# Transposing u in 32x32 blocks on VectorE and through memory instead of on TensorE, in the last layer of a retention and feed-forward kernel

## The chip, the cores and the metric

One core of a Trainium2 chip. The core has a matrix engine (TensorE; in the profile PE, and PEld for its weight loads), VectorE (DVE), ScalarE (ACT), GpSimd (POOL) and SyncE (SP, which only issues DMAs), an on-chip memory of 128 partitions (SBUF), accumulation banks that TensorE writes (PSUM), and 16 DMA engines that move data between SBUF and DRAM (HBM). The metric is the time of one execution on the device in microseconds, the median of several runs.

## The reference

Three layers follow each other. Retention over 4 batches of 8 heads gives 3072 tokens of 512 values; a first feed-forward layer follows, and then the layer that this change touches:

```python
def _moe2_ref(x, w_in, w_out, g_ln) -> np.ndarray:   # x 3072 x 512, w_in 512 x 1024, w_out 1024 x 512
    h = x @ w_in
    h_max = np.max(h, axis=-1, keepdims=True)
    e = np.exp(h - h_max)
    sm = e / (np.sum(e, axis=-1, keepdims=True) + 1e-09)
    solu = h * sm
    mu = np.mean(solu, axis=-1, keepdims=True)
    var = np.mean((solu - mu) ** 2, axis=-1, keepdims=True)
    ln = (solu - mu) / np.sqrt(var + 1e-06) * g_ln
    return (ln @ w_out).astype(np.float32)
```

All data is float32. The kernel multiplies float32 operands as pairs of rounded halves: each operand is split into a high part and a rest, and three products (high by high, high by rest, rest by high) are summed.

## The kernel before

The kernel is written so that TensorE's order stands in the code; the order on the other engines is made by a scheduler when the program is built, and each engine then runs its list strictly in that order, waiting where an operand is not there. The DMAs that SyncE issues are such a list too, and so are those that ScalarE issues in between its computations.

The first two layers fill the time up to about 606 us. The last layer works on 24 tiles of 128 tokens (P = 128), in 12 pairs; pair j holds the tiles 2j and 2j + 1, called the even and the odd tile below. For each pair:

- h2, the product with w_in, is formed in seven partial products (a scheme that saves one of eight) of 6 matmuls each, 42 in all. `part` issues them; `keep2` and `add_half` bring the sums from PSUM into a tile `hn` of 128 x 1024 and find its maximum. The odd tile's `hn` is complete after P4, the even one's after P3, the last of the seven.
- `soft` makes u from it: the exponential on ACT (line 951), the product h·exp with its row sum on DVE (line 953), the mean subtracted from it on DVE (line 955), the sum of squares on ACT (line 957), and some one-column operations for the scale.
- `trans` turns u: 8 transposes of 128 x 128 on TensorE into PSUM (line 976, tiles `ptr`), a rounded copy `uh` on ACT (line 978), and the rest `ul` on DVE (line 979). After it the 1024 inner values lie on the partitions, in 8 blocks of 128.
- `outp` multiplies by w_out: 24 matmuls of 512 columns (line 990), the eviction with the scale on ACT (line 996) and the output's DMA, issued by ACT (line 998).

`load_y` fetches the layer's input `yl` from DRAM two or three pairs ahead (line 469, issued by SyncE); `sum_y` and `split_y` form the sums and the rounded parts of it on POOL and ACT (lines 476, 483 to 486 and 499).

The pair 0 is computed inside the last steps of the layer before. Then a loop over j from 1 to 12 puts TensorE's work in this order: P1 and P2 of pair j, the transposes of the odd tile of pair j - 1, P6 and P5, the transposes of its even tile, P7, the first half of the odd tile's output, P4 and P3, the rest of that output, and the even tile's output. In j = 12 there is no pair left and only transposes and outputs remain.

Of the kernel before, what the change touches and what calls it, by code (L numbers as in the profile page):

```python
# [60 lines left out]
C_MASK = C_HALF + 1  # L61
C_IDENT = C_MASK + D
C_END = C_IDENT + P

# [6 lines left out]
def constants():  # L71
    gamma = 1.0 - 2.0 ** (-5.0 - np.arange(H, dtype=np.float64))
    i = np.arange(P, dtype=np.float64)
    out = np.zeros((P, C_END), np.float64)
    out[:, C_IDENT : C_IDENT + P] = np.eye(P)
    for c in range(NC):
        out[:, C_VS + c * H : C_VS + (c + 1) * H] = gamma[None, :] ** -(c * P + i[:, None] + 1)
    out[:, C_HALF] = -0.5
    out[:, C_MASK : C_MASK + D] = np.tile(i[:D, None] <= i[None, :D], (2, 1))

    tab = np.zeros((NC, P, NP * P), np.float64)
    of_q = tab.reshape(NC, 2, D, NP, P)
    for p in range(NP):
        for h in range(2):
            for c in range(NC):
                of_q[c, h, :, p, :] = gamma[2 * p + h] ** (c * P + i + 1) / np.sqrt(D)
    return out.astype(np.float32), tab.astype(np.float32)
# [3 lines left out]
def body(ctx: ExitStack, tc, z, w_in, w_out, w_in2, w_out2, g_ln, cst, tab, out):  # L91
# [19 lines left out]

    con = cpool.tile([P, C_IDENT], F32, name="con")
    gl = cpool.tile([P, NF2], F32, name="gl")
# [5 lines left out]
    gd = {s: yd.tile([P, NF1, SB], F32, name=f"gd{s}") for s in range(2, NSB)}  # L119
    y1d = [yd.tile([P, B, NK, P], F32, name=f"y1d{s}") for s in range(NSB)]  # L120


# [499 lines left out]
    load_tab(0)  # L622
    nc.scalar.dma_start(out=con, in_=cst[:, :C_IDENT])
    load_half(0, 1)
# [283 lines left out]
    w2p = ctx.enter_context(tc.tile_pool(name="w2p", bufs=7))  # L908
    bp = ctx.enter_context(tc.tile_pool(name="bp", bufs=1))
    sp = ctx.enter_context(tc.tile_pool(name="sp", bufs=3))  # L910
    ident = bp.tile([P, P], F32, name="ident")
    nc.sync.dma_start(out=ident, in_=cst[:, C_IDENT:])
    uc, ut, sc2, po_of = {}, {}, {}, {}

# [31 lines left out]
    def soft(i, h, last):  # L946
# [7 lines left out]
        nc.vector.tensor_scalar(us, us, -1.0 / FF2, None, ALU.mult)  # L954
        nc.vector.tensor_scalar(hn, ex, us, None, ALU.add)
        ssq = sp.tile([P, 1], F32, tag="ssq", name="ssq")
        nc.scalar.activation(ex, hn, AF.Square, accum_out=ssq)

# [7 lines left out]
        uc[i], sc2[i] = hn, sc  # L966

    def trans(i):
        u = uc.pop(i)
        uh = t4([P, NF2, P], F32R, "uh")  # L970
        ul = t4([P, NF2, P], F32R, "ul")
        for half in range(2):
            pt_ = ps_t.tile([P, 4, P], F32, tag="tr", name="ptr")
            for q in range(4):
                f = 4 * half + q
                nc.tensor.transpose(pt_[:, q, :], u[:, f * P : (f + 1) * P], ident)  # L976
            hs = slice(4 * half, 4 * half + 4)
            nc.scalar.copy(uh[:, hs, :], pt_)
            nc.vector.tensor_tensor(ul[:, hs, :], pt_, uh[:, hs, :].bitcast(F32), ALU.subtract)
        ut[i] = (uh, ul)  # L980

    def outp(i, fs):
        uh, ul = ut[i]
        if fs[0] == 0:
            po_of[i] = ps_o.tile([P, DM], F32, tag="o", name="po")
        po = po_of[i]
        for f in fs:
            bh, bl = dec2.w[f]
            for n, (a, b) in enumerate(((uh, bh), (uh, bl), (ul, bh))):
                nc.tensor.matmul(  # L990
                    po, a[:, f, :], b, start=f == 0 and n == 0, stop=f == NF2 - 1 and n == 2
                )
        if fs[-1] < NF2 - 1:
            return
        ob = t2([P, DM], F32, "ob")
# [45 lines left out]
    for n, (s, f) in enumerate(steps):  # L1041
# [19 lines left out]
        if s == NSB - 1:  # L1061
# [14 lines left out]
            if f == 12:  # L1076
                split_y(1)
            if f == 14:
                sum_y(2)
# [3 lines left out]

    ps_2 = ctx.enter_context(tc.tile_pool(name="ps_2", bufs=4, space=PSUM, reuse_waits="tile"))
    ps_t = ctx.enter_context(tc.tile_pool(name="ps_t", bufs=2, space=PSUM, reuse_waits="tile"))
    ps_o = ctx.enter_context(tc.tile_pool(name="ps_o", bufs=2, space=PSUM, reuse_waits="tile"))
    NJ = NTT // 2
    bank_of[:] = [(ps_2, "h2")]
    load_y(3)
    with tc.manual_schedule(engines={mybir.EngineType.PE}):  # L1090
        for j in range(1, NJ + 1):
            if j + 1 < NJ:
                split_y(j + 1)
            a, b = 2 * j - 1, 2 * j - 2
            pair = Pair(j) if j < NJ else None

            def parts2(*ms):
                for m in ms if pair else ():
                    pair.part(m)

            parts2(P1, P2)
            trans(a)
            parts2(P6, P5)
            trans(b)
            if j + 2 < NJ:
                sum_y(j + 2)
            if j + 3 < NJ:
                load_y(j + 3)
            parts2(P7)
            outp(a, range(4))  # L1110
            parts2(P4, P3)
            outp(a, range(4, NF2))
            outp(b, range(NF2))

# [54 lines left out]
```

## Time and profile before

| | us |
|---|---|
| median of 3 runs | 875.61 (874.99 to 877.58) |
| the profiled execution's own time | 874.27 |
| its span in the trace | 872.5 |
| TensorE busy in the span | 840.5 (96%) |
| VectorE, ScalarE, GpSimd busy | 540.0, 438.8, 303.6 |
| TensorE's granted clock, mean over the span | 0.993 of full speed |

The span runs from the first to the last instruction of the traced execution; the 1.8 us around it belong to the start and the end of the program. A matmul that is queued behind another overlaps it in the trace, so the mean duration of one is longer than the distance from one to the next; the distances are what counts for the time.

### The profile page before, as it was taken

Reading aid. Unit: us, or ns where it says so; the run is one execution under the profiler, and the core shown is the slowest. Engines: PE = TensorE matmul, PEld = TensorE weight load, DVE = VectorE, ACT = ScalarE, POOL = GpSimd, SP = SyncE. Lnnn points to the kernel's source line nnn. Section 1 sums busy time; section 2 is a strip of 40 time slices with the busy share of each in tenths; the row PEclk is TensorE's granted clock in tenths of the full one; section 3 lists DMA queues with packets and bytes.
Section 4 is the critical chain, followed back from the end, with each engine's and each line's share of the span. In section 5 each row is a group of like instructions: output and inputs, shape, how many; then the busy total and the mean of one; then the engine's idle time right before and its main releaser. Section 6 shows DMA issues by size and latency. Waiting matters only on the chain.

```text
span 872.5 us, 16642 instructions
## 1 busy us (share of the span) xinstructions
PE 840.5 (96%) x6488; PEld 693.8 (80%) x6488; DVE 540.0 (62%) x1023; ACT 438.8 (50%) x868; POOL 303.6 (35%) x304
## 2 busy tenths in 40 slices
PE   5799999999999899999999999999899999999997
PEld 5678888888877687887788888888788888888886
DVE  3788876999768766224465977555455545544441
ACT  4656643646545455445453445435555555555442
POOL 4521100271634257343300430235644444444200
PEclk9999999999999899999999999999999999999999
DMA  9668754335899528935676455522111111100001
GB/s 363 252 236 298 241 203 152 113 134 213 305 361 331 181 80 283 410 143 173 242 276 211 152 199 208 188 105 76 58 49 49 49 48 48 45 30 25 22 17 47
DMA packets 66462, 144.34 MB, mean 165 GB/s; under 512 B 6608, under 2 KB 19024, under 8 KB 66384
## 3 DMA queue, kind: packets, MB, share of 16 engines
q1 hardware_dynamic: 58032, 128.28, 41.7%
q10 hardware_dynamic: 8352, 15.00, 4.6%
q8 instruction: 51, 0.84, 0.4%
q14 instruction: 27, 0.22, 0.1%
HBM read 94.50 MB, written 48.76 MB: 164 GB/s over the span
## 4 chain that ended last, share of the span: by engine, by line
PE 82%; DMA 5%; DVE 4%; issue 3%; POOL 3%; ACT 2%; SPq 0%; ACTq 0%; POOLq 0%; DVEq 0%
PE py L378 28%; PE po L990 15%; PE ph L751 12%; PE ph L926 12%; PE ph L353 8%; PE ptr L976 2%; DMA z<-z 2%; PE out L229 2%; PE sc L229 2%; DMA raw<-w_in 1%; POOL hs L769 1%; DMA wcd<-wch 1%; DMA wf<-wod 1%; POOL yls L476 1%; DVE wf L145 1%
## 5 line engine op out<-in xcount | busy, mean ns | idle before, releaser
L378 PE MATMUL py<-gp,w 128*128 128x512 f32 x768 | 175.4, 389 | 0.0
L378 PEld LDWEIGHTS py<-gp,w 128*128 128x128 f32 x768 | 144.2, 188 | 29.9
L990 PE MATMUL po<-w,uh 128*128 128x512 f32 x384 | 118.6, 390 | 0.0
L769 POOL TENSOR_TENSOR hs<-hs,th 128x512 f32<-128x512 f32 x48 | 66.5, 1389 | 97.1 <-ACT th L767 86.9
L476 POOL TENSOR_TENSOR yla<-yl,yha 128x256 fp32r<-128x256 f32 x36 | 40.0, 1140 | 130.7 <-ACT yha L499 130.7
L990 PEld LDWEIGHTS po<-w,uh 128*128 128x128 f32 x384 | 72.1, 188 | 14.9
L353 PE MATMUL ph<-xh,w 128*128 128x512 f32 x256 | 82.2, 395 | 0.9 <-DVE w L155 0.9
L378 PE MATMUL py<-gh,w 128*128 128x512 f32 x256 | 79.3, 390 | 0.3 <-ACT gh L366 0.3
L990 PE MATMUL po<-w,ul 128*128 128x512 f32 x192 | 74.9, 390 | 0.0
L154 ACT CAST w<-wf 128x512 fp32r<-128x512 f32 x70 | 43.0, 619 | 58.4 <-DVE wf L145 47.7
L926 PE MATMUL ph<-w,yhs 128*128 128x512 f32 x192 | 61.3, 400 | 0.0
L767 ACT ACTIVATE th<-hs 128x512 f32<-128x512 f32 x48 | 30.3, 631 | 61.2 <-DVE hs L777 54.7
L162 DVE TENSOR_TENSOR gp<-g,gp 128x512 fp32r<-128x512 f32 x64 | 48.7, 772 | 19.6 <-ACT gp L161 19.4
L155 DVE TENSOR_TENSOR w<-wf,w 128x512 fp32r<-128x512 f32 x70 | 51.3, 738 | 15.1 <-ACT w L154 14.3
L751 PE MATMUL ph<-xh,wch 128*128 128x512 f32 x140 | 57.3, 409 | 1.6 <-DVE hs L777 1.6
L353 PEld LDWEIGHTS ph<-xh,w 128*128 128x128 f32 x256 | 48.0, 188 | 11.8 <-DVE w L155 1.3
L378 PEld LDWEIGHTS py<-gh,w 128*128 128x128 f32 x256 | 48.0, 188 | 10.6 <-ACT gh L366 0.7
L751 PE MATMUL ph<-xl,wch 128*128 128x512 f32 x140 | 55.4, 396 | 0.0
L751 PE MATMUL ph<-xh,wcl 128*128 128x512 f32 x140 | 55.2, 395 | 0.0
L777 DVE TENSOR_TENSOR hs<-ph,part 128x512 f32<-128x512 f32 x48 | 33.0, 687 | 35.3 <-PE ph L751 20.9
L951 ACT ACTIVATE ex<-hn,nm 128x1024 f32<-128x1024 f32 x24 | 27.7, 1153 | 53.2 <-DVE nm L941 52.4
L751 PE MATMUL ph<-xh,wc 128*128 128x512 f32 x168 | 53.2, 391 | 1.2 <-ACT part L761 0.6
(124 smaller groups left out, 1777.6 us busy)
## 6 DMA issues: line engine op xcount, KB each, us to landing
z<-z SPq DMA_DIRECT2D x48, 512.0 KB, 7.2
g<-gd SPq DMA_DIRECT2D x64, 256.0 KB, 5.4
raw<-w_in SPq DMA_DIRECT2D x24, 512.0 KB, 6.2
raw<-w_out SPq DMA_DIRECT2D x24, 512.0 KB, 4.5
gd<-hs SPq DMA_DIRECT2D x48, 256.0 KB, 3.8
y1d<-ysb SPq DMA_DIRECT2D x24, 256.0 KB, 3.5
wc<-wcd SPq DMA_DIRECT2D x12, 512.0 KB, 6.6
yl<-y1d SPq DMA_DIRECT2D x12, 512.0 KB, 4.0
```

The costliest lines, as they stand in the source:

```text
L154: pin(nc.scalar.copy(hi, wf), fixed)
L155: pin(eng.tensor_tensor(lo, wf, hi.bitcast(F32), ALU.subtract), fixed)
L162: eng.tensor_tensor(o, src, h.bitcast(F32), ALU.subtract)
L229: pin(nc.tensor.matmul(o, a, b, start=True, stop=True, skip_group_check=True), held[0])
L353: nc.tensor.matmul(ph, a[:, k, :], x, start=n == 0, stop=n == 3 * NK - 1), s < 2
L378: nc.tensor.matmul(py[e], a[:, cols], x, start=f == 0 and n == 0, stop=f == NF1 - 1 and n == 2)
L476: nc.gpsimd.tensor_tensor(out[:, at], a[:, at], b[:, at], op)
L751: nc.tensor.matmul(ph, a, x, start=first and n == 0, stop=n == 5, skip_group_check=True)
L769: eng.tensor_tensor(g, h, th, ALU.subtract)
L777: nc.vector.tensor_tensor(h, ph, part, ALU.add)
L926: nc.tensor.matmul(ph, x[:, r, :], w, start=first and n == 0, stop=n == 5, skip_group_check=True)
L990: nc.tensor.matmul(po, a[:, f, :], b, start=f == 0 and n == 0, stop=f == NF2 - 1 and n == 2)
```

## The change

TensorE's transposes go. In `soft` ACT now subtracts the mean (an Identity activation with the mean as its bias, in place of DVE's line 955), and the sum of squares is taken from the unshifted product with the same bias. DVE then transposes the tile within blocks of 32 x 32 (`nc.vector.transpose`, into the buffer `ex`), and SyncE stores it to a DRAM tensor `ud` (512 KB, 4 KB contiguous from each partition). A new step `turn` reads it back into `hn` with another order of rows: each destination partition gathers 32 runs of 32 values (128 bytes each), 4096 runs for a tile. `trans` then makes `uh` and `ul` from that in SBUF, with one copy on ACT and one subtraction on DVE of 128 x 1024 each. The rows of w_out and g_ln are reordered on the host to match, and the identity matrix goes.

The order on TensorE is new too: all 42 matmuls of pair j run together, and behind them the 48 output matmuls of pair j - 1. At the end the matmuls of pairs 10 and 11 follow each other, and then the outputs of the pairs 9, 10 and 11. The PSUM banks of the transposes go to h2 (6 instead of 4).

```diff
--- before.py
+++ after.py
...
@@ -118,6 +116,7 @@
     wcd = [[yd.tile([P, 4, 256], F32, name=f"wcd{j}_{i}") for i in range(4)] for j in range(NJ1)]
     gd = {s: yd.tile([P, NF1, SB], F32, name=f"gd{s}") for s in range(2, NSB)}
     y1d = [yd.tile([P, B, NK, P], F32, name=f"y1d{s}") for s in range(NSB)]
+    ud = [yd.tile([P, NF2 * P], F32, name=f"ud{i}") for i in range(NTT)]
 
 
     def raw_load(src):
...
@@ -952,9 +948,12 @@
         us = sp.tile([P, 1], F32, tag="us", name="us")
         nc.vector.scalar_tensor_tensor(ex, hn, 1.0, ex, ALU.mult, ALU.mult, accum_out=us)
         nc.vector.tensor_scalar(us, us, -1.0 / FF2, None, ALU.mult)
-        nc.vector.tensor_scalar(hn, ex, us, None, ALU.add)
+        nc.scalar.activation(hn, ex, AF.Identity, bias=us)
         ssq = sp.tile([P, 1], F32, tag="ssq", name="ssq")
-        nc.scalar.activation(ex, hn, AF.Square, accum_out=ssq)
+        nc.scalar.activation(ex, ex, AF.Square, bias=us, accum_out=ssq)
+
+        nc.vector.transpose(ex, hn)
+        nc.sync.dma_start(out=ud[i], in_=ex)
 
         nc.vector.tensor_scalar(ssum, ssum, 1e-9, -1.0, ALU.add, ALU.mult)
         nc.vector.reciprocal(ssum, ssum)
@@ -965,33 +964,28 @@
         nc.gpsimd.tensor_tensor(sc, sc, ssum, ALU.mult)
         uc[i], sc2[i] = hn, sc
 
+    def turn(j):
+        for i in (2 * j + 1, 2 * j):
+            nc.sync.dma_start(
+                out=uc[i].rearrange("p (c i b) -> p c i b", c=NF2, i=B),
+                in_=ud[i].rearrange("(i a) (g c b) -> (a g) c i b", i=B, g=4, c=NF2),
+            )
+
     def trans(i):
         u = uc.pop(i)
-        uh = t4([P, NF2, P], F32R, "uh")
-        ul = t4([P, NF2, P], F32R, "ul")
-        for half in range(2):
-            pt_ = ps_t.tile([P, 4, P], F32, tag="tr", name="ptr")
-            for q in range(4):
-                f = 4 * half + q
-                nc.tensor.transpose(pt_[:, q, :], u[:, f * P : (f + 1) * P], ident)
-            hs = slice(4 * half, 4 * half + 4)
-            nc.scalar.copy(uh[:, hs, :], pt_)
-            nc.vector.tensor_tensor(ul[:, hs, :], pt_, uh[:, hs, :].bitcast(F32), ALU.subtract)
-        ut[i] = (uh, ul)
-
-    def outp(i, fs):
-        uh, ul = ut[i]
-        if fs[0] == 0:
-            po_of[i] = ps_o.tile([P, DM], F32, tag="o", name="po")
-        po = po_of[i]
-        for f in fs:
+        uh, ul = (t4([P, NF2 * P], F32R, "u" + n) for n in "hl")
+        parts(uh, ul, u, nc.vector)
+        ut[i] = [w.rearrange("p (f t) -> p f t", f=NF2) for w in (uh, ul)]
+
+    def outp(i):
+        uh, ul = ut.pop(i)
+        po = ps_o.tile([P, DM], F32, tag="o", name="po")
+        for f in range(NF2):
             bh, bl = dec2.w[f]
             for n, (a, b) in enumerate(((uh, bh), (uh, bl), (ul, bh))):
                 nc.tensor.matmul(
                     po, a[:, f, :], b, start=f == 0 and n == 0, stop=f == NF2 - 1 and n == 2
                 )
-        if fs[-1] < NF2 - 1:
-            return
         ob = t2([P, DM], F32, "ob")
         nc.scalar.activation(ob, po, AF.Copy, scale=sc2.pop(i))
         at = i % B * S + i // B * P
@@ -1075,42 +1069,51 @@
                 pair.part(m)
             if f == 12:
                 split_y(1)
+            if f == 13:
+                turn(0)
             if f == 14:
                 sum_y(2)
     G.close()
     M.close()
 
 
-    ps_2 = ctx.enter_context(tc.tile_pool(name="ps_2", bufs=4, space=PSUM, reuse_waits="tile"))
-    ps_t = ctx.enter_context(tc.tile_pool(name="ps_t", bufs=2, space=PSUM, reuse_waits="tile"))
+    ps_2 = ctx.enter_context(tc.tile_pool(name="ps_2", bufs=6, space=PSUM, reuse_waits="tile"))
     ps_o = ctx.enter_context(tc.tile_pool(name="ps_o", bufs=2, space=PSUM, reuse_waits="tile"))
     NJ = NTT // 2
     bank_of[:] = [(ps_2, "h2")]
     load_y(3)
+
+    def pair_of(j, before):
+        pair = Pair(j)
+        for n, m in enumerate((P1, P2, P6, P5, P7, P4, P3)):
+            if n == 0 and j + 1 < NJ:
+                split_y(j + 1)
+            if n == 2 and j + 2 < NJ:
+                sum_y(j + 2)
+            if n == 4 and j + 3 < NJ:
+                load_y(j + 3)
+            if n == 5 and before is not None:
+                trans(2 * before + 1)
+            pair.part(m)
+        turn(j)
+        if before is not None:
+            trans(2 * before)
+
+    def outs(j, after=None):
+        for half in (1, 0):
+            outp(2 * j + half)
+            if after is not None:
+                trans(2 * after + half)
+
     with tc.manual_schedule(engines={mybir.EngineType.PE}):
-        for j in range(1, NJ + 1):
-            if j + 1 < NJ:
-                split_y(j + 1)
-            a, b = 2 * j - 1, 2 * j - 2
-            pair = Pair(j) if j < NJ else None
-
-            def parts2(*ms):
-                for m in ms if pair else ():
-                    pair.part(m)
-
-            parts2(P1, P2)
-            trans(a)
-            parts2(P6, P5)
-            trans(b)
-            if j + 2 < NJ:
-                sum_y(j + 2)
-            if j + 3 < NJ:
-                load_y(j + 3)
-            parts2(P7)
-            outp(a, range(4))
-            parts2(P4, P3)
-            outp(a, range(4, NF2))
-            outp(b, range(NF2))
+        for j in range(1, NJ - 1):
+            pair_of(j, j - 1)
+            if j < NJ - 2:
+                outs(j - 1)
+        pair_of(NJ - 1, None)
+        outs(NJ - 3, NJ - 2)
+        outs(NJ - 2, NJ - 1)
+        outs(NJ - 1)
 
 
 def kernel(q, k, v, moe_w_in, moe_w_out, moe2_w_in, moe2_w_out, moe2_g_ln):
@@ -1149,8 +1152,12 @@
         "w_in2": words(
             moe2_w_in.reshape(NK, P, 2, 512).transpose(0, 2, 1, 3).reshape(2 * NK, P, 512)
         ),
-        "w_out2": words(moe2_w_out.reshape(NF2, P, DM)),
-        "g_ln": np.ascontiguousarray(moe2_g_ln.reshape(NF2, P).T),
+        "w_out2": words(
+            moe2_w_out.reshape(4, NF2, P // 4, DM).transpose(1, 2, 0, 3).reshape(NF2, P, DM)
+        ),
+        "g_ln": np.ascontiguousarray(
+            moe2_g_ln.reshape(4, NF2, P // 4).transpose(2, 0, 1).reshape(P, NF2)
+        ),
         "cst": cst,
         "tab": tab,
     }
```

The order on ACT in the last layer, before: one period, from the copies of the even tile of pair 3 to the sums of squares of pair 4 (`ptr` is a transposed half tile in PSUM, `po` an output in PSUM, `yl` and `ysum` the input of a pair to come).

```order
L978 CAST uh_7604<-ptr_7606 128x512
L978 CAST uh_7604<-ptr_7613 128x512
L933 COPY part_7633<-ph2_7556 128x512
L951 ACTIVATE ex_7657,ssum_7658<-hn_7550,nm_7551 128x1024
L951 ACTIVATE ex_7680,ssum_7681<-hn_7553,nm_7555 128x1024
L499 CAST yha_7739<-yl_7422 128x512
L499 CAST yha_7739<-yl_7422 128x256
L996 ACTIVATE ob_7708<-po_7636,sc_7467 128x512
L499 CAST yhs_7741<-ysum_7620 128x1024
L998 DMA out<-ob_7708 128x512
L957 ACTIVATE ex_7657,ssq_7664<-hn_7550 128x1024
L957 ACTIVATE ex_7680,ssq_7687<-hn_7553 128x1024
```

And after the change, the same period, from the copy of the odd tile of pair 3 on (`hn_7319` and `hn_7322` are the odd and the even tile of pair 3, gathered back from DRAM; `hn_7504` and `hn_7507` those of pair 4).

```order
L160 CAST uh_7572<-hn_7319 128x1024
L947 ACTIVATE ex_7584,ssum_7585<-hn_7504,nm_7505 128x1024
L947 ACTIVATE ex_7609,ssum_7610<-hn_7507,nm_7509 128x1024
L160 CAST uh_7629<-hn_7322 128x1024
L951 ACTIVATE hn_7504<-ex_7584,us_7587 128x1024
L498 CAST yha_7695<-yl_7376 128x512
L498 CAST yha_7695<-yl_7376 128x256
L953 ACTIVATE ex_7584,ssq_7591<-ex_7584,us_7587 128x1024
L498 CAST yhs_7697<-ysum_7541 128x1024
L951 ACTIVATE hn_7507<-ex_7609,us_7612 128x1024
L990 ACTIVATE ob_7658<-po_7633,sc_7414 128x512
L953 ACTIVATE ex_7609,ssq_7616<-ex_7609,us_7612 128x1024
```

The copies that made `uh` in halves from PSUM are now two whole ones, which read what the DMAs brought back; the second stands behind both exponentials and ahead of the two shifts of the mean, which are new on ACT.

SyncE's list in the last layer, before: the input loads only.

```order
L469 DMA yl_7016<-y1d2_133 128x1024
L469 DMA yl_7219<-y1d2_133 128x1024
L469 DMA yl_7422<-y1d3_134 128x1024
L469 DMA yl_7625<-y1d3_134 128x1024
L469 DMA yl_7828<-y1d4_135 128x1024
```

And after, for the pairs 3 and 4: a store of the odd tile, its gather, the store of the even tile, an input load, the gather of the even tile.

```order
L956 DMA ud7_144<-ex_7399 128x1024
L969 DMA hn_7319<-ud7_144 128x32x32
L956 DMA ud6_143<-ex_7424 128x1024
L468 DMA yl_7561<-y1d3_134 128x1024
L969 DMA hn_7322<-ud6_143 128x32x32
L956 DMA ud9_146<-ex_7584 128x1024
L969 DMA hn_7504<-ud9_146 128x32x32
L956 DMA ud8_145<-ex_7609 128x1024
L468 DMA yl_7746<-y1d4_135 128x1024
L969 DMA hn_7507<-ud8_145 128x32x32
```

The gather of a tile waits for its own store to land, and the next store stands behind that wait in the list. So the two tiles of a pair go out and come back one after the other, with an input load in between.

## Rows read from the trace of the kernel before

**Rows 1.** The profile's page: the span, and part 1 (busy time, share and instructions per engine):
```profile
span 872.5 us, 16642 instructions
PE 840.5 (96%) x6488; PEld 693.8 (80%) x6488; DVE 540.0 (62%) x1023; ACT 438.8 (50%) x868; POOL 303.6 (35%) x304
```

**Rows 2.** Chain that ended last, in order of time (start us, us): a steady period, then the end:
```profile
743.27 2.72 PE ph L926 x12
746.00 0.87 PE ptr L976 x8
746.87 2.74 PE ph L926 x12
749.62 0.87 PE ptr L976 x8
750.49 1.38 PE ph L926 x6
751.87 2.74 PE po L990 x12
754.61 2.72 PE ph L926 x12
757.34 8.16 PE po L990 x36
765.49 2.72 PE ph L926 x12
...
857.66 10.94 PE po L990 x48
```

**Rows 3.** The last stage: busy time of each engine; who PE waited for (total, times, longest):
```profile
core 0: us, PE busy (x) PEld busy (x) DVE busy (x) ACT busy (x) POOL busy (x), PEclk, DMA share, GB/s
606.50:868.60 262.10, 258.53 (x1231) 214.69 (x1230) 126.67 (x319) 130.29 (x222) 108.01 (x160) 1.00 0.13 44
...
PE ptr L976 <- DVE ul L979: 3.5, 2, 2.4
```

**Rows 4.** Timeline of ACT in that steady period (start us, us; idle before in brackets):
```profile
756.87 1.15 ACT L951 ACTIVATE ex<-hn,nm 128x1024 f32<-128x1024 f32 x1 [4.37 <-DVE nm L941]
758.23 1.16 ACT L951 ACTIVATE ex<-hn,nm 128x1024 f32<-128x1024 f32 x1
759.38 0.91 ACT L499 CAST yha<-yl 128x512 fp32r<-128x512 f32 x2
760.78 1.04 ACT L499 CAST yhs<-ysum 128x1024 fp32r<-128x1024 f32 x1
763.07 1.06 ACT L957 ACTIVATE ex<-hn 128x1024 f32<-128x1024 f32 x1
```

**Rows 5.** Groups by line between 715 and 760 us (busy us, mean ns of one):
```profile
L953 DVE SCALAR_TENSOR_TENSOR ex<-hn,ex 128x1024 f32<-128x1024 f32 x5 | 6.1, 1226 | 0.2
L979 DVE TENSOR_TENSOR ul<-ptr,uh 128x512 fp32r<-128x512 f32 x8 | 5.2, 686 | 5.1 <-ACT uh L978 5.1
...
L996 ACT ACTIVATE ob<-po,sc 128x512 f32<-128x512 f32 x4 | 2.7, 686 | 2.6 <-PE po L990 2.6
```

**Rows 6.** DMA queues in 607.0:609.0, 700.4:701.3 and 716.3:718.7 us (packets, MB, share of 16 engines):
```profile
q1 hardware_dynamic: 1147, 0.57, 101.1%
...
q10 hardware_dynamic: 144, 0.26, 77.7%
...
q1 hardware_dynamic: 132, 0.50, 74.3%
```

**Rows 7.** SyncE's issues that touch y1d (ns min/median/max), and output DMAs (us to landing):
```profile
L389 SPq DMA_DIRECT2D y1d<-ysb x24: 512/573/2367, 236.3 to 608.1; - x24
L469 SPq DMA_DIRECT2D yl<-y1d x12: 319/320/589, 542.7 to 759.9; - x12
...
out<-ob ACTq DMA_DIRECT2D x24, 256.0 KB, 2.0
```

**Rows 8.** Timeline of DVE where the last stage begins:
```profile
607.46 1.30 DVE L955 TENSOR_SCALAR hn<-ex,us 128x1024 f32<-128x1024 f32 x1
```

More of the change, by code (lines that the diff above doesn't have):

```diff
@@ L61 @@
 C_MASK = C_HALF + 1
-C_IDENT = C_MASK + D
-C_END = C_IDENT + P
+C_END = C_MASK + D
 def col(p, h):
@@ L74, in constants @@
     out = np.zeros((P, C_END), np.float64)
-    out[:, C_IDENT : C_IDENT + P] = np.eye(P)
     for c in range(NC):
@@ L110, in t2 @@
         return mid.tile(shape, dtype, tag="t2", name=name)
-    con = cpool.tile([P, C_IDENT], F32, name="con")
+    con = cpool.tile([P, C_END], F32, name="con")
     gl = cpool.tile([P, NF2], F32, name="gl")
@@ L622, in body @@
     load_tab(0)
-    nc.scalar.dma_start(out=con, in_=cst[:, :C_IDENT])
+    nc.scalar.dma_start(out=con, in_=cst)
     load_half(0, 1)
@@ L908, in body @@
     w2p = ctx.enter_context(tc.tile_pool(name="w2p", bufs=7))
-    bp = ctx.enter_context(tc.tile_pool(name="bp", bufs=1))
     sp = ctx.enter_context(tc.tile_pool(name="sp", bufs=3))
-    ident = bp.tile([P, P], F32, name="ident")
-    nc.sync.dma_start(out=ident, in_=cst[:, C_IDENT:])
-    uc, ut, sc2, po_of = {}, {}, {}, {}
+    uc, ut, sc2 = {}, {}, {}
     def bank2():
```

## The prediction

> **What bounds the kernel now.** I read the page first: TensorE is busy 840.5 of 872.5 us, every other engine at most 62% [rows 1]. Then the chain of waits in order of time, for the stretch that the change touches, the last layer: in a steady period it is TensorE alone, from the first partial product of one pair (743.27) to that of the next (765.49), 22.22 us [rows 2]. The reader should see there what a pair costs: 2.72 + 2.74 + 1.38 + 2.72 = 9.56 us for the 42 matmuls of h2, 2.74 + 8.16 = 10.90 us for the 48 of the outputs, and 0.87 us for each of two groups of eight transposes. Third, busy time over the whole stage, 606.5 to 868.6: TensorE is idle for 262.1 - 258.5 = 3.6 us only, nearly all of it waits of transposes [rows 3]; VectorE is busy 127 and ScalarE 130 of 262. So time leaves this stage only if TensorE loses work, and it stays away only if what replaces that work is never waited for.
>
> **What is removed.** With 11 pairs of h2 and 12 of outputs in the stage, the matmuls that stay take 11 x 9.56 + 12 x 10.90 = 236.0 us. The stage takes 262.1 [rows 3], so 26.1 us go if TensorE then never waits: 24 x 0.87 = 20.9 of transposes, 3.5 of waits, 1.7 of gaps around them. A period becomes 9.56 + 10.90 = 20.46 us. That is the gain at most.
>
> **What is added on the engines.** Per tile, ACT gets a shift of the mean (1.06, as the pass over 128x1024 of line 957 [rows 4]) and a whole copy (1.04, as the line 499 row of the same size) and loses two half copies from PSUM. VectorE loses the shift and two subtractions of 0.69 and gets a transposition and one subtraction of 128x1024. For the transposition no row exists; the nearest is another pass of VectorE over 128x1024, 1.23 us [rows 5], and I take 1.2, with twice that as the upper bound. Both engines are about half busy, so their sums fit into a period; only their order and their waits matter.
>
> **What is added on the DMA queue.** Here is the unknown price. A gather moves 4096 runs of 128 bytes, 256 for each of 16 engines. No transfer of the trace has such runs in number. While only 512-byte runs flowed (607.0 to 609.0), the queue was full with 1147 packets; 32 of them are the short semaphore writes of two finished transfers, so one run took 2.0 x 1.011 x 16 / 1115 = 29.0 ns. While an output of 2 KB rows flowed, 0.9 x 0.777 x 16 / 128 = 87.4 ns [rows 6]. The line through both is 9.5 ns plus 0.038 ns per byte. It gives 14.4 ns for 128 bytes, or 3.7 us for a gather. The bounds are 9.5 ns (a run without length, 2.4 us) and 29.0 ns (a short run costs what 512 bytes cost, 7.4 us). I take the line, since the time of a run grows nearly in proportion to its bytes between the two rows.
>
> The Trainium skill speaks against that: "DMA: Bandwidth & Descriptors", section Specifications, wants 512 bytes or more for line rate, and says that below this the engine reads, modifies and writes. By that rule a run costs no less than a 512-byte one, and the time would be that of the third case below; by the row's line it is the forecast. No run here shows which.
>
> The rest of a transfer: an output of 256 KB lands 2.0 us after its issue [rows 7], 0.7 of it data, so 1.3 us are fixed. A store of 512 KB then takes 1.3 + 8 x (9.5 + 0.038 x 4096) ns = 2.6 us, a gather 1.3 + 3.7 = 5.0. SyncE's own issue is 0.32 us for a load with 128 runs and at least 0.51 for a store with 512 [rows 7], so 0.5 ns per run, and 2.3 us for a gather.
>
> **The loop that must stay under 20.46 us.** TensorE's order gives u a whole period to come back. But on ACT the copy of the even gathered tile stands between the exponentials of the next pair and the two shifts of the mean. If that gather is late, the next pair's chain is late too, and the delay returns each period. So I add it up from the start of that copy: copy 1.04, shift of the odd tile 1.06, two copies of the input 0.91, squares 1.1 [rows 4]: 4.1. Transposition 1.2: 5.3. The store lands at 7.9 and the odd gather is issued; SyncE is free at 10.2; that gather lands at 12.9. Meanwhile ACT has done 1.04, the even shift 1.06, an eviction 0.69 [rows 5] and the squares 1.1, and VectorE the even transposition: ready at 9.2. The even store is issued at 10.2, but its data stand behind the odd gather in the same queue: landed at 12.9 + 1.3 = 14.2. Then the even gather: 14.2 + 5.0 = 19.2. The input load ahead of it holds the engines for 2.4 x 0.743 = 1.8 us [rows 6], mostly during the even gather's fixed part, and two outputs of 0.7 pass: 1.2 us together. Semaphores between engines: 0.2. The loop is 20.6 us, just over TensorE's 20.46. With the price p of a run in ns it is 20.6 + 0.512 (p - 14.4), since both gathers are in it. There are nine such loops (the even gathers of pairs 0 to 8 to those of 1 to 9); at the end three pairs of outputs, 32.7 us of matmuls, cover what is left.
>
> **The start of the stage.** The even tile of pair 0 is late already: VectorE shifts it until 608.76 [rows 8], behind the evictions of the layer before. Shifted and transposed about 1.5 us later, its store queues with the input stores that flow until past 609 [rows 6], and the odd gather after it lands at about 616.5. Its copy and subtraction (1.04 + 2 x 0.69) end at 619, where TensorE is ready at 606.5 + 9.6 = 616.1. I put 3 us on this, between 0 and 8.
>
> **The sum.** 872.5 - 26.1 + 3.0 + 9 x 0.14 = 850.7 us of span. The profiled execution took 1.8 us more than its span: 852.5. It is 1.3 us below the median of the runs shown, 875.61: so 854 us.
>
> **The rivals.**
> - *The gathers are only partly hidden.* Each ns on p costs 9 x 0.512 = 4.6 us, and so does a slower transposition: at 2.4 us the odd chain grows by 1.2, or 11 us. With p = 17 the loop is 21.9 and the time 854 + 12 = 866. For it: the margin in the loop is nil, and six steps of it have prices from other rows. Against it: the row for the output's fixed part is the median of 24. The Trainium skill, "VectorE: DVE Perf Modes", section The three transpose paths, gives 311 ns for 128x128 in bf16; eight of those would be 2.5 us, an estimate, and the time 866 as well.
> - *Slower: SyncE's chain sets the period.* A short run costs what a 512-byte run costs, 29.0 ns. The loop is 20.6 + 0.512 x 14.6 = 28.1 us, against 22.22 before, and the time 854 + 9 x 7.5 = 921. It decides from p = 19.1 on, where the 21.6 us gained are given back in nine loops of 2.4. For it: the odd gather, the even store, the load and the even gather pass one queue one after the other, and two waits for a landing lie between them. Against it: the two rows on which the line rests.
> - *No change that can be seen*: gain and loss meet, p between 18.5 and 19.7.
>
> **How the numbers follow.** Hidden or nearly so (p up to about 15): 0.46, with 849 to 858 us. Partly hidden: 0.19. No change: 0.06, within 0.3% or 2.6 us of 875.6, about what a measurement of this kernel can tell. Slower: 0.29. So faster 0.65, same 0.06, slower 0.29. The forecast is the first case, 854. Below, the range ends at 848, where neither the start nor the loops cost anything (about 0.05 left out). Above, it takes in the partly hidden cases and the slower ones up to p = 25 (loop 26.0): 854 + 9 x 5.4 = 903, so 904, with about 0.15 above.
>
> **What the profile after would show.** Right: no `ptr` rows; a period of 20.4 to 20.7 us from one pair's first matmul to the next; `hn<-ud` landing about 5 us after its issue; ACT's copy of the even tile starting without idle time. Wrong, if the period is over 21 us, PE waits at line 986 or 922 for what ACT and DVE make, and ACT's largest wait is for `hn<-ud`: then the queue's share of the 16 engines tells the price of a run. A period of 20.46 with a total near 875 would mean that the time was lost at the start or the end.

## The result, and the profile after

The changed kernel takes 866.8 us (median of 4 runs, 865.54 to 868.64) against 875.33 us (874.99 to 877.58) of the kernel before on the same chip: a ratio of 0.990, interval 0.987 to 0.992. It is faster, by 8.5 us. The forecast was 854, so of 21.6 us foreseen 8.5 came.

From the page of the kernel after (span; busy time per engine; the larger group of h2's matmuls; the two transfers of the transposition):

```profile
span 865.4 us, 16366 instructions
PE 829.4 (96%) x6296; PEld 675.4 (78%) x6296; DVE 540.7 (62%) x999; ACT 461.2 (53%) x868; POOL 291.6 (34%) x304
...
L922 PE MATMUL ph<-w,yhs 128*128 128x512 f32 x192 | 63.9, 416 | 6.4 <-ACT part L929 5.8
...
ud<-ex SPq DMA_DIRECT2D x24, 512.0 KB, 4.5
hn<-ud SPq DMA_DIRECT2D x24, 512.0 KB, 5.8
```

Against [rows 1] TensorE lost 11 us of busy time only, and the span 7. The `ptr` groups are gone, yet TensorE now waits for ACT's copies of the partial products (`part`) behind line 922.

The chain of waits of the kernel after, in order of time (start, us, what), for one period, answers to [rows 2]:

```profile
655.70 6.81 PE ph L922 x30
...
662.53 0.60 ACT part L929
...
663.15 0.69 DVE hn L937
...
663.91 1.66 PE ph L922 x6
665.57 11.11 PE po L986 x48
```

Where [rows 2] had TensorE alone, the chain leaves it once a period: after P7 (30 matmuls) it runs over ACT's copy and VectorE's `add_half` and comes back at P3 (the 6 matmuls). P3 adds to the bank of P5, which `add_half` must have read first. P4 lies between, but is only 1.36 us long. The next period starts at 676.67, after 20.97 us; without any wait it would take 20.40, as counted below. Of the 0.57 us between, 0.35 is lost up to the first output matmul, at P3. The other 0.22 is lost right behind: the third output matmul of the odd tile needs `ul`, which VectorE makes only after `add_half` (timeline of the same period):

```profile
664.68 1.22 DVE L161 TENSOR_TENSOR ul<-hn,uh 128x1024 fp32r<-128x1024 f32 x1
...
665.95 0.19 PEld L986 LDWEIGHTS po<-w,ul 128*128 128x128 f32 x1 [0.36 <-DVE ul L161]
```

Later periods are longer, and there the chain goes through a gather and both engines behind it:

```profile
769.83 5.95 DMA hn<-ud
...
775.81 1.06 ACT uh L160
...
776.89 1.23 DVE ul L161
...
778.19 5.30 PE po L986 x22
```

Two places remain, the first and the last pair of the stage. The timelines of ACT and TensorE there (start, us; idle before, and who ended it):

```profile
611.77 1.04 ACT L498 CAST yhs<-ysum 128x1024 fp32r<-128x1024 f32 x1 [2.28 <-POOL ysum L485]
612.72 0.58 ACT L929 COPY part<-ph 128x512 f32<-128x512 f32 x1
613.35 1.22 PE L922 MATMUL ph<-w,yhs 128*128 128x512 f32 x2 [3.41 <-ACT part L929]
```

```profile
817.92 1.04 ACT L160 CAST uh<-hn 128x1024 fp32r<-128x1024 f32 x1 [1.16 <-DMA hn<-ud]
818.87 0.58 ACT L929 COPY part<-ph 128x512 f32<-128x512 f32 x1
...
819.50 0.72 PE L922 MATMUL ph<-w,yhs 128*128 128x512 f32 x2 [2.35 <-ACT part L929]
```

In both it is P6, behind P1 and P2, that waits: it adds to the bank of P1, which ACT's copy `part` must have read first. ACT was free to make that copy, but stood at an instruction ahead of it in its list: at the start the split of a later input, which waits for GpSimd, at the end the copy of an even tile whose outputs come 16 us later and whose gather was still under way. Behind both, the granted clock fell to half for some microseconds. The windows show it (columns: length, busy time of PE, PEld, DVE, ACT, POOL, clock, DMA share, GB/s):

```profile
613.00:619.00 6.00, 5.65 (x13) 4.46 (x14) 0.70 (x2) 0.88 (x2) 6.00 (x10) 0.50 1.17 228
...
820.00:824.00 4.00, 4.00 (x12) 3.09 (x12) 2.50 (x8) 3.97 (x6) 0.46 (x1) 0.57 0.03 13
```

All of it can be counted in one way. In two kernels below (best2 and bnotr), a period of 90 matmuls without any wait takes 20.40 us, 0.2267 each. What a stretch takes beyond its matmuls at that price is lost. The stretches are: start (pair 1's first matmul to pair 2's), steady (eight periods, to pair 10's), end (to the last output matmul). In the changed kernel they lose 7.2, 6.6 and 5.0 us, 18.8 together; the forecast's sum had 3.0 for the start and 1.3 for the loops, 4.3. The difference, 14.5, is nearly what the span is off: 865.4 against the 850.7 of the sum. (One execution of the kernel `start` in the table below ran at a granted clock of 0.56 throughout, in 1369 us, and is left out.)

### The profile page after: what moved, and what is told of

It is laid out like the page before. It is cut to its first block, busy times and chain, and to the rows that moved or that the text cites. A ratio compares the mean times of both kernels' runs of the same rounds, so it can differ in the third digit from the quotient of the medians.

```text
span 865.4 us, 16366 instructions
## 1 busy us (share of the span) xinstructions
PE 829.4 (96%) x6296; PEld 675.4 (78%) x6296; DVE 540.7 (62%) x999; ACT 461.2 (53%) x868; POOL 291.6 (34%) x304
## 4 chain that ended last, share of the span: by engine, by line
PE 81%; DVE 5%; DMA 4%; ACT 3%; issue 3%; POOL 2%; SPq 0%; ACTq 0%; POOLq 0%; DVEq 0%
PE py L377 29%; PE ph L750 15%; PE po L986 14%; PE ph L922 11%; PE ph L352 8%; PE out L228 2%; DMA hn<-ud 2%; PE sc L228 2%; DMA z<-z 1%; DMA raw<-w_in 1%; ACT part L929 1%; POOL hs L768 1%; DVE hn L937 1%; POOL yls L475 1%; ACT uh L160 0%
## 5 line engine op out<-in xcount | busy, mean ns | idle before, releaser
L922 PE MATMUL ph<-w,yhs 128*128 128x512 f32 x192 | 63.9, 416 | 6.4 <-ACT part L929 5.8
L475 POOL TENSOR_TENSOR yla<-yl,yha 128x256 fp32r<-128x256 f32 x36 | 26.3, 756 | 127.2 <-ACT yha L498 127.2
L937 DVE CUSTOM_DVE_ANT_0 hn<-ph,part 128x512 f32<-128x512 f32 x24 | 16.6, 691 | 72.5 <-ACT part L929 54.9
L154 DVE TENSOR_TENSOR w<-wf,w 128x512 fp32r<-128x512 f32 x70 | 51.2, 736 | 15.3 <-ACT w L153 14.5
L161 DVE TENSOR_TENSOR gp<-g,gp 128x512 fp32r<-128x512 f32 x64 | 48.4, 770 | 18.8 <-ACT gp L160 18.6
L929 ACT COPY part<-ph 128x512 f32<-128x512 f32 x36 | 21.1, 586 | 64.7 <-PE ph L922 64.7
```

The source lines that it names most:

```text
L154: pin(eng.tensor_tensor(lo, wf, hi.bitcast(F32), ALU.subtract), fixed)
L161: eng.tensor_tensor(o, src, h.bitcast(F32), ALU.subtract)
L475: nc.gpsimd.tensor_tensor(out[:, at], a[:, at], b[:, at], op)
L922: nc.tensor.matmul(ph, x[:, r, :], w, start=first and n == 0, stop=n == 5, skip_group_check=True)
```

## The experiments

The theory was that the transposes' time did leave TensorE and the price of the short runs was near the forecast, and that the gain went into waits which the new order makes. The rival was that the gathers, by their runs or their queue, take it back. The table has every kernel; the times are medians in us, and the kernel before took 874.7 to 875.7 on the chips of these runs. The ratios are to the kernel before on the same chip. The losses are those of one traced execution each; for `start` that is the single one described below.

| kernel | time | ratio to before | start | steady (period) | end |
|---|---|---|---|---|---|
| changed | 866.8 | 0.990 (0.987 to 0.992) | 7.2 | 6.6 (21.23) | 5.0 |
| contig: contiguous gathers | 863.2 | 0.987 (0.985 to 0.989) | 6.2 | 4.6 (20.98) | 3.3 |
| fill: 6 matmuls held back | 860.2 | 0.984 (0.982 to 0.986) | 7.2 | 4.1 (20.91) | 2.2 |
| start: input split later | 865.9 | 0.990 (0.988 to 0.992) | 6.9 | 6.9 (21.27) | 5.0 |
| end: a copy later | 863.0 | 0.987 (0.986 to 0.989) | 6.2 | 6.7 (21.24) | 2.4 |
| fill12: 12 held back | 857.4 | 0.980 (0.977 to 0.983) | 4.8 | 1.7 (20.62) | 2.3 |
| all2: fill12, end spread | 860.7 | 0.983 (0.981 to 0.986) | 5.9 | 1.5 (20.59) | 5.4 |
| runs64: runs of 64 bytes | 921.2 | 1.052 (1.048 to 1.056) | 9.7 | 45.0 (26.03) | 17.4 |
| best: fill12, two edits at the start | 866.9 | 0.990 (0.987 to 0.993) | 6.3 | 9.6 (21.60) | 2.4 |
| best2: the same, old queue order | 855.5 | 0.977 (0.974 to 0.979) | 6.4 | 0.0 (20.40) | 2.3 |
| border: before, new neighbourhood | 878.9 | 1.003 (1.001 to 1.005) | | (22.57) | |
| bnotr: before, no transposition | 851.3 | 0.974 (0.971 to 0.977) | | (20.40) | |

**Contiguous gathers.**

```diff
-                out=uc[i].rearrange("p (c i b) -> p c i b", c=NF2, i=B),
-                in_=ud[i].rearrange("(i a) (g c b) -> (a g) c i b", i=B, g=4, c=NF2),
+                out=uc[i],
+                in_=ud[i],
```

> The gather reads the stored tile as 128 runs of 4 KB instead of 4096 runs of 128 bytes; the order of everything stays as in the changed kernel. It leaves out the exchange of the 32x32 blocks, so the output is not the reference's. Theory (the time was given back mostly by waits that the new order makes on TensorE and ACT, and the runs' price was near the forecast): the period stays near 20.97 us, because the wait between P4 and P3 remains, and only the 2 to 2.5 us of loops and part of the 5 us at the end go: 3 to 6 us faster than the changed kernel, 861 to 864 us. Rival (the short runs and the DMA queue take the gain back): the period falls to 20.5 us and the time to 853 to 856 us.

863.2 us: 3.6 less than the changed kernel (2.5 by the ratios), inside the theory's bounds and far from the rival's. The groups of ACT from 640 to 805 us, of the changed kernel and of this one:

```profile
L160 ACT CAST uh<-hn 128x1024 fp32r<-128x1024 f32 x16 | 16.8, 1051 | 8.8 <-DMA hn<-ud 8.8
```

```profile
L160 ACT CAST uh<-hn 128x1024 fp32r<-128x1024 f32 x16 | 16.7, 1044 | 0.0
```

ACT's wait for the gathers is gone, and with it 2.0 of the 6.6 us lost in the steady stretch. The other 4.6 stay: every period takes 20.97 or 21.0 us, with no late gather in it. So the two losses of 0.35 and 0.22 us, at P3 and for `ul`, do not come from the short runs.

**Six output matmuls between P4 and P3.** Of each even tile, f = 6 and 7 are held back to the next pair.

```diff
             pair.part(m)
+            if n == 5 and j > 1 and before is not None:
+                outp(2 * before - 2, range(6, NF2))
...
-            outp(2 * j + half)
+            outp(2 * j + half, range(6) if half == 0 and after is None and j < NJ - 3 else range(NF2))
```

> Six of the 24 output matmuls of each even tile (f 6 and 7, tiles of pairs 0 to 8) are held back and issued between P4 and P3 of the pair after the next. Theory: the wait of P3 for add_half behind P7 (0.60 of ACT and 0.69 of VectorE against 1.36 us of P4) costs about 0.5 us a pair and is covered now: nine pairs, 4 to 4.5 us, so 862 to 863 us, with a period of 20.5 us. Rival (the loop through the two gathers sets the period by itself): the wait only moves from P3 to the first output matmul or to P1, the period stays at 20.9 to 21.2 us and the time at 866 to 867 us.

860.2 us, faster than either expected, but the period stayed at 20.91, as the rival said: what went is the late gathers and the end (5.0 to 2.2), where the gathered tile was back when ACT came to its copy, and the copy of P1 behind it kept TensorE waiting for 0.2 us only. The chain of a period tells why:

```profile
690.53 1.04 ACT hn L951
691.57 0.94 ACT uh L160
...
692.54 1.24 DVE ul L161
...
693.82 3.96 PE po L990 x16
697.78 6.81 PE ph L922 x30
```

P3 no longer waits. Now the first outputs of the even tile do, for `ul`. That comes from ACT's copy of the even tile, which stands behind both exponentials and a shift, and these hang on P7. The rival was right on the period and wrong on the loop: no DMA is in this chain.

**Twelve held back**, six between P4 and P3 and six behind P3. Against the kernel with six:

```diff
-            if n == 5 and j > 1 and before is not None:
-                outp(2 * before - 2, range(6, NF2))
+            if n > 4 and j > 1 and before is not None:
+                outp(2 * before - 2, range(2 * n - 6, 2 * n - 4))
...
-            outp(2 * j + half, range(6) if half == 0 and after is None and j < NJ - 3 else range(NF2))
+            outp(2 * j + half, range(4) if half == 0 and after is None and j < NJ - 3 else range(NF2))
```

> Twelve output matmuls of each even tile are held back to the next pair, six between P4 and P3 and six behind P3. With six held back the period stayed at 20.92 us although P3 no longer waited: the chain from P7 through both exponentials, a shift of the mean and the copy of the even tile to its outputs came back after 30 + 18 matmuls. Theory: with six matmuls more outside that chain (1.36 us) it needs 19.6 us, and TensorE alone sets the period: 20.46 us, nine periods by 0.46 = 4 us under the kernel with six held back, 856 us. Rival (the loop through both gathers, forecast at 20.6 us and of 20.9 to 21.7 us in the changed kernel, sets it now): the period stays over 20.8 us and the time at 859 to 860 us.

857.4 us, within the spread of the theory's 856. From pair 3 on every period takes 20.40 us. Busy time from 640 to 800 us, the changed kernel ahead of this one, shows TensorE idle for 0.6 us here, all at 652, ahead of the first period of 20.40:

```profile
640.00:800.00 160.00, 158.94 (x678) 125.34 (x677) 84.87 (x200) 102.33 (x151) 64.98 (x106) 1.00 0.64 143
```

```profile
640.00:800.00 160.00, 159.41 (x702) 131.38 (x701) 88.56 (x206) 106.94 (x159) 67.62 (x112) 1.00 0.69 152
```

The count in brackets tells more than the busy time, which overlapping matmuls fill: 702 matmuls in place of 678.

**The new neighbourhood in the kernel before**, transposes and all.

```diff
             parts2(P7)
-            outp(a, range(4))
             parts2(P4, P3)
-            outp(a, range(4, NF2))
+            outp(a, range(NF2))
```

> The kernel before the change, transposes on TensorE and all, with one thing of the new order: the twelve output matmuls that stood between P7 and P4 of a pair come behind P3, so that P7, P4 and P3 follow one another. Theory (this neighbourhood costs TensorE a wait of about 0.5 us a pair, with no transfer in it): 11 pairs, 5 to 6 us slower than before, 880 to 881 us, with a period of 22.7 instead of 22.22 us. Rival (the new wait of the changed kernel comes from its slower chain through memory, not from the neighbourhood): 874 to 877 us.

878.9 us; by the ratio 2.9 above before (1.1 to 4.6). The period grew from 22.22 to 22.57, and the chain shows the same detour as in the changed kernel, with no transfer anywhere:

```profile
756.94 0.59 ACT part L933
...
757.56 0.69 DVE hn L941
...
758.31 1.66 PE ph L926 x6
```

The sign is the theory's; the size is 0.35 us a pair, below its 0.5. It is what P3 loses in the changed kernel too. The 0.22 us for `ul` are not in this kernel, whose copies and subtractions of the odd tile come much earlier.

**The transposes alone.** The kernel before, where `trans` reads `u` itself:

```diff
-            pt_ = ps_t.tile([P, 4, P], F32, tag="tr", name="ptr")
-            for q in range(4):
-                f = 4 * half + q
-                nc.tensor.transpose(pt_[:, q, :], u[:, f * P : (f + 1) * P], ident)
             hs = slice(4 * half, 4 * half + 4)
+            pt_ = u.rearrange("p (f t) -> p f t", f=NF2)[:, hs, :]
```

> The kernel before the change with the transposes on TensorE left out and nothing in their place: ACT copies and VectorE subtracts from u itself, in halves as before; the order of the rest is the old one. It leaves out the transposition of u, so the output is not the reference's. Theory (the transposes and the waits for them were worth the 26.1 us of the forecast, and the old order, with twelve output matmuls between P7 and P4, has no other wait): 848 to 851 us and a period of 20.46 us. Rival (without the transposes the chain through ACT and VectorE to the outputs is waited for, in the old order too): a period over 20.8 us and 853 to 858 us.

851.3 us, 24.2 less than before (20 to 26 by the ratio's interval), with every period at 20.40. The two waits left are in the first pair (3.6 us). So the 26.1 us of the forecast were worth 24.2, in an order with cover behind P7.

**Runs of 64 bytes.**

```diff
-            nc.sync.dma_start(
-                out=uc[i].rearrange("p (c i b) -> p c i b", c=NF2, i=B),
-                in_=ud[i].rearrange("(i a) (g c b) -> (a g) c i b", i=B, g=4, c=NF2),
-            )
+            to = uc[i].rearrange("p (c i b) -> p c i b", c=NF2, i=B)
+            at = ud[i].rearrange("(i a) (g c b) -> (a g) c i b", i=B, g=4, c=NF2)
+            for h in range(2):
+                nc.sync.dma_start(out=to[..., 16 * h : 16 * h + 16], in_=at[..., 16 - 16 * h : 32 - 16 * h])
```

> Each gather of the changed kernel is made of two transfers with 4096 runs of 64 bytes each, where it had 4096 runs of 128. It leaves the halves of each 32-element run swapped, so the output is not the reference's. A run's price by the line of the forecast is 9.5 + 0.038 x 64 = 11.9 ns, two are 23.9, against 13.2 measured for one of 128 bytes. Theory (the loop through both gathers is only just hidden, as the forecast had it, 0.512 us for each ns): a loop grows by 5.5 us, the period to 26 to 27 us and the time to about 915 us. Rival (the gathers have several us of slack, or a run of 64 bytes costs half of one of 128): the period stays under 22 us and the time under 880 us.

921.2 us and a period of 26.0 on average: the theory. The rows of the DMA queue give the prices: in the changed kernel from 677.5 to 679.5 us, and here from 740.2 to 741.5, while hardly anything but these runs flowed:

```profile
q1 hardware_dynamic: 2711, 0.35, 111.5%
```

```profile
q1 hardware_dynamic: 2100, 0.13, 109.2%
```

A run of 128 bytes took 2.0 x 1.115 x 16 / 2711 = 13.2 ns, one of 64 took 1.3 x 1.092 x 16 / 2100 = 10.8. Two of those are 8.4 ns dearer than one of 128, which at 0.512 us per ns is 4.3 us a loop; the period grew by 4.8. The run also doubles the gathers that SyncE issues, and no run separates that from the price of the runs.

**The end.** ACT's copy of the even tile of pair 9 comes behind P7 of the last pair.

```diff
+            if n == 5 and before is None:
+                trans(2 * (j - 2))
...
-        if before is not None:
+        if before is not None and j < NJ - 2:
             trans(2 * before)
```

> ACT's copy of the even tile of pair 9 is issued behind P7 of the last pair instead of ahead of its P1. Theory: the copy of P1 of the last pair no longer waits for that tile's gather, the idle stretch of 2.4 us at 817 and the fall of the granted clock behind it go: 4 to 5 us, 862 to 863 us. Rival (another wait takes its place within the last pair, such as P3 for add_half, or the outputs for the copy that now comes later): under 1.5 us go, 865 to 867 us.

863.0 us, 3.8 less (2.3 by the ratios), nearly the theory's. The idle stretch at 817 and the fall of the clock behind it are gone, and the end loses 2.4 us in place of 5.0; of these 0.8 is a wait for ACT's copy within the last pair, as its rival said.

**The end, spread** (with twelve held back and the edit above): the odd outputs of pair 9 in part ahead of and within the last pair.

```diff
+            if n > 4 and before is None:
+                outp(2 * j - 3, range(2 * n - 6, 2 * n - 4))
...
+        outp(2 * NJ - 5, range(4))
         pair_of(NJ - 1, None)
```

> As with twelve held back, and at the end the copy of the even tile of pair 9 comes behind P7 of the last pair, and the 24 output matmuls of the odd tile of pair 9 are spread: twelve ahead of the last pair, six between its P4 and P3, six behind. Theory: the waits in the last pair, 1.5 to 3 us in the kernels so far, go as well: 853 to 855 us, that is the forecast of 854 plus nothing but the start. Rival: what is left at the end is paid in the outputs behind, and the time is that of twelve held back within 1 us.

860.7 us, 3.3 worse than twelve held back, against both. The timeline near the end shows the outputs of the last pair:

```profile
845.42 1.04 ACT L160 CAST uh<-hn 128x1024 fp32r<-128x1024 f32 x1 [5.61 <-DMA hn<-ud]
...
846.52 0.73 PE L990 MATMUL po<-w,uh 128*128 128x512 f32 x2 [1.57 <-ACT uh L160]
```

The outputs moved forward were the cover of the last pair's own way through memory.

**The start.**

```diff
-            if n == 0 and j + 1 < NJ:
+            if n == (5 if j == 1 else 0) and j + 1 < NJ:
                 split_y(j + 1)
```

In the text of the first pair the split now stands between P7 and P4.

> In the first pair of the stage ACT splits the input of the next pair after P4's place in the order instead of ahead of P1, so the copy of P1 no longer stands behind a copy that waits for GpSimd. Theory: the idle stretch of 3.4 us at 609.6 goes and the granted clock stays at full speed until 619, so about 6 us go, 860 to 862 us. Rival (the first gathers are late anyway, and the wait comes back at the first outputs or at the next P1): the idle time only moves by a few us, 865 to 867 us.

865.9 us, as the changed kernel: the rival. Where the time goes is read from one more execution:

> The kernel with the later split of the input in the first pair once more, for its profile: it measured 866.3 us, no gain. Theory: the 3.4 us of idle time at P2 are gone, and TensorE waits as long at the first outputs instead, for the odd gather of the first pair, which lands at about 618 us because its store is queued behind the input stores of the stage before. Rival: ACT's first copy still waits, for something else than the input, and the idle stretch is where it was.

```profile
609.94 0.63 SPq L969 DMA_DIRECT2D hn<-ud  x1
...
616.52 1.04 ACT L160 CAST uh<-hn 128x1024 fp32r<-128x1024 f32 x1 [1.96 <-DMA hn<-ud]
...
617.62 0.74 PE L986 MATMUL po<-w,uh 128*128 128x512 f32 x2 [2.27 <-ACT uh L160]
```

It took 864.3 us. The wait behind P2 shrank to 0.55 us, and TensorE waits 2.27 us at the first output instead, then 1.04 for `ul`: the first odd gather, issued at 609.94, lands at 616.5. The start lost 6.9 us against 7.2.

**Twelve held back, with two edits at the start**: the one above, and the first odd store on ACT's queue.

```diff
-        nc.sync.dma_start(out=ud[i], in_=ex)
+        (nc.scalar if i == 1 else nc.sync).dma_start(out=ud[i], in_=ex)
```

> Twelve held-back matmuls, and at the start the split of the input behind P4's place as well as the store of the first odd tile on ACT's own queue, not behind the input stores on SyncE's. Theory: the 3.4 us of idle time at P2 go, and the first odd gather lands at 616 instead of 618 us, so that the wait at the first outputs is 2 instead of 4 us: 2 to 3 us under twelve held back, 854 to 856 us. Rival (both queues share the 16 engines, and the store's data flow as late as before): 857 us, as with twelve held back.

866.9 us, 9.6 worse (8.5 by the ratios), which neither allowed for. Most of the loss is not at the start (6.3 in place of 4.8 us) but in the steady periods (9.6 in place of 1.7; a period of 21.60). SyncE's issues in one period, of twelve held back and of this kernel:

```profile
653.73 0.33 SPq L956 DMA_DIRECT2D ud<-ex  x1
...
657.03 0.59 SPq L969 DMA_DIRECT2D hn<-ud  x1
657.71 2.81 SPq L956 DMA_DIRECT2D ud<-ex  x1
660.62 0.37 SPq L468 DMA_DIRECT2D yl<-y1d  x1
...
663.95 0.59 SPq L969 DMA_DIRECT2D hn<-ud  x1
```

```profile
653.48 0.33 SPq L956 DMA_DIRECT2D ud<-ex  x1
653.85 0.46 SPq L468 DMA_DIRECT2D yl<-y1d  x1
655.18 0.32 SPq L956 DMA_DIRECT2D ud<-ex  x1
656.42 5.45 SPq L969 DMA_DIRECT2D hn<-ud  x2
```

The scheduler, given the split at another place, had reordered the lists for all periods: on SyncE both stores and the load now go ahead of the odd gather, and on ACT both shifts ahead of the first squares. The last run has the split one step later (n == 6), which leaves the old sequence in every period:

> The run before it lost 9.6 us against twelve held back, and its SyncE queue carries, in every period, both stores and the input load ahead of the two gathers (store, load, store, gather, gather), where the others carry store, gather, store, load, gather. Here the split of the input in the first pair stands one step later, behind P4 and ahead of P3's own step in the text, which leaves SyncE's old sequence in every period; the store of the first odd tile stays on ACT's queue. Theory (the sequence on SyncE cost the 9.6 us, since the odd gather then waits for the even store, and the two edits at the start are worth 2 to 3 us): 854 to 856 us and no waits between 660 and 800 us. Rival (the two edits at the start cost something themselves in every period): 862 us or more.

855.5 us, and from 640 to 800 us TensorE is never idle:

```profile
640.00:800.00 160.00, 160.00 (x707) 132.57 (x706) 88.21 (x206) 105.75 (x158) 70.13 (x116) 1.00 0.69 148
```

The sequence had cost the 9.6 us of the steady periods (which part SyncE's list and which part ACT's, no run separates). The edits at the start gave nothing by themselves: the start lost 6.4 us, where twelve held back lost 4.8 and 1.7 in the period behind; the stage took 243.8 us against 243.9. The difference of 1.8 us in time is not clear of the noise: the intervals of the two ratios overlap.

## Why the prediction was wrong

*What is removed* was right. TensorE lost the transposes, and in an order with cover (bnotr) that is worth 24.2 us of the 26.1; the period of 20.46 was measured as 20.40.

*The price of a run* was right: 14.4 ns by the line, 13.2 measured. The Trainium skill's rule in "DMA: Bandwidth & Descriptors", section Specifications, that below 512 bytes the engine reads, modifies and writes, would, as the prediction read it, have made it no cheaper than the 29.0 ns of [rows 6]; the traces don't agree, for these DRAM to SBUF reads. *The transposition* took 1.25 us, forecast 1.2:

```profile
L955 DVE STREAM_TRANSPOSE ex<-hn 128x1024 f32<-128x1024 f32 x20 | 24.9, 1246 | 33.9 <-ACT ex L953 33.9
```

The estimate from the Trainium skill, "VectorE: DVE Perf Modes", section The three transpose paths, was 2.5; the measurement, of blocks of 32x32 in float32, decides against it.

*The loop* was the right mechanism and a little too short: 20.6 us, where periods with the gather in their chain took up to 21.7. runs64 bears out the slope (4.3 us by the prices, 4.8 measured). Nine loops were put at 1.3 us; the gathers cost 2.0 in eight. A gather landed 5.8 us after its issue, forecast 5.0. SyncE's issue of a gather was wrong (0.59 us, not 2.3), but the store behind it then stands for 2.6 to 3.0, so the chain came out alike.

**The step that failed is "26.1 us go if TensorE then never waits"**: the sum took that condition as met but for 4.3 us, and TensorE loses 18.8 to waits and to the clock behind them.

- *The neighbourhood of P7, P4 and P3* was not looked at. The old order had twelve output matmuls there, and the forecast counted them only as part of a pair's 10.90 us of outputs. Missing: 0.57 us a period, 4.6 of the steady stretch. The larger part, 0.35 at P3, is shown by border without any transfer; the other 0.22, the wait of the first outputs for `ul`, stands in contig too. With twelve matmuls held back both are gone.
- *The end* was put at nothing, since "three pairs of outputs, 32.7 us of matmuls, cover what is left". They cover what stands on TensorE. ACT's list was not followed: the copy of a tile needed only later stood ahead of P1's copy. The end lost 5.0 us, of which the run end took away 2.6.
- *The start* had 3 us, between 0 and 8, for a late gather; 7.2 were measured, inside that span but by another wait: P6 for ACT's copy of P1, with 6 us at half the clock behind it. With the idle time behind P2 gone (start_look) about the same time is lost at the first outputs, so the late gather of the forecast is there, landing at the 616.5 foreseen, but hidden behind the first wait. What the clock adds differs between runs. No run here brings the start near 3 us.

The rival "partly hidden" gave 866, and the time is 866.8. That it fits is an accident: its reason was a dearer run or transposition, and neither happened; with contiguous gathers 863.2 remain. The signs of being wrong that the prediction named did show, a period over 21 us (21.23) and waits at line 922, but it took them to point to the price of a run. best2, without loss in the steady periods and with 2.3 us at the end, runs at 855.5, 1.5 us above the forecast; its span of 855.2 is 4.5 above the sum's 850.7, and its losses of 8.7 are 4.4 above the sum's.

## What to carry to other kernels

When an order is rewritten, list for each accumulation or buffer what lies between its last reader and its next writer, before and after; work that is "only moved" may have been the cover of a chain. When a wait is named after an engine that had time, look at the instruction ahead of it in that engine's list. And a local edit under a scheduler can change every period, so compare the lists of the queues as well as the place that was edited.

## What the runs showed of the hardware that was not expected

- Issues behind a gather are held up on SyncE: the gather itself takes 0.59 us there, the store behind it 2.57 us in place of the 0.32 of a free one:

```profile
655.05 0.58 SPq L969 DMA_DIRECT2D hn<-ud  x1
655.99 2.57 SPq L956 DMA_DIRECT2D ud<-ex  x1
```

- An idle stretch does not always bring the clock down: after 3.4 us of idle time behind P2 the changed kernel ran at half speed until 619 (the row of 613 to 619 us above), twelve held back, after the same idle time, at full speed; no run shows why:

```profile
617.00:623.00 6.00, 5.84 (x25) 4.53 (x26) 1.39 (x5) 1.53 (x3) 5.65 (x10) 1.00 1.18 217
```

- GpSimd's subtraction `yla` between 640 and 850 us takes 741 ns, before the change 1223. The transposes of TensorE are not the reason, since bnotr, which has none, takes 1218. In before, border and bnotr each of these subtractions runs at the same time as VectorE's shift of the mean (line 955 there); in the changed kernel, where that shift is on ACT, those beside VectorE's transposition take no longer than the others. The groups of GpSimd in bnotr, then in the changed kernel:

```profile
L476 POOL TENSOR_TENSOR yla<-yl,yha 128x256 fp32r<-128x256 f32 x24 | 28.6, 1218 | 72.2 <-ACT yha L499 72.2
```

```profile
L475 POOL TENSOR_TENSOR yla<-yl,yha 128x256 fp32r<-128x256 f32 x24 | 17.1, 741 | 86.7 <-ACT yha L498 86.7
```
